# One column of a weight matrix, read at the start on GpSimd's DMA queue and not used

## The chip, the cores and the metric

The kernel runs on one core of a Trainium2 chip. A core has five engines with an instruction stream each: TensorE (PE, matmuls and transposes), VectorE (DVE), ScalarE (ACT), GpSimd (POOL) and SyncE (SP). DMAs are issued by SyncE, ScalarE and GpSimd into queues of their own, which sixteen DMA engines serve. The metric is the device time of one execution in microseconds; less is better.

## The reference

Two stages. The first is a linear recurrence over time for 4 batches x 8 heads, with states of 48 x 48; the second takes its output as 3,072 tokens of 384 numbers through two matmuls with a squared ReLU between them.

```
# r, k, v: (4, 8, 768, 48);  w, u: (8, 48)
for t in range(768):
    cur   = einsum('bhd,bhe->bhde', u * k_t, v_t)
    y_t   = einsum('bhd,bhde->bhe', r_t, state + cur)
    state = w * state + einsum('bhd,bhe->bhde', k_t, v_t)
x = y as (3072, 384)
h = x @ w_in                  # w_in:  (384, 2048)
out = max(h, 0)**2 @ w_out    # w_out: (2048, 384)
```

## The kernel before, in words

**Tiling.** Time is cut into 6 chunks of 128 steps. A unit is one chunk of one batch: 24 units, unit i = 4 x chunk + batch. Within a chunk the recurrence becomes matmuls: r and k are scaled by powers of w (step `scale`), turned so that the head dimension lies on the partitions (`turn`, `rkT` for units 0 to 5; a DMA transpose, `rkD`, from unit 6 on), multiplied with each other (`at`), masked to the lower triangle (`mask`), and multiplied by v (`y`); a diagonal term with u comes from `d` and `dv`, and the carried state from `s`, `sadd`, `sdec`, `stb`. The output of a unit, `yb`, is turned again (`xturn`, `xT`, or by DMA, `xD`), and goes through the first matmul (`m1`), ReLU and square (`relu`, `sqA` on ScalarE, `sqD` on VectorE), the second matmul (`m2`), a copy (`osb`) and a store (`out`).

**Order.** Each engine runs its instructions in the order in which the kernel writes them. That order is one long list of step names, `ORDER`; the loop at the end of the kernel walks it and calls the function of each step. A step name carries its unit, and `rt.1.1` is the second half of r of unit 1 (four heads of it). `fill.N` stands for N matmuls of a constant tile that nobody reads; they keep PE busy while it has nothing to do.

**Start.** Ahead of the list stands a prologue. ScalarE issues the loads of w, spread over partitions (`wrow`), and of half of r of unit 0; VectorE makes constants from `iota_i`, a column of partition numbers that GpSimd writes (L164); GpSimd sets the small tile `wu` and loads w and u into it (L166 to L169). The first steps of the list are then

```
kt.0.0 kt.0.1 rt.0.0 rt.1.0 I.0 rt.1.1 vt.0 ktA.1.0 lnat.0 fill.26 log@4567 kt.1.1 lnat.1 ids rt.2.0 w.1 upper w.0
fill.8 cols@1 rt.2.1 wk scale.0.0 kt.2.0 zeros scale.0.1 wr fill.8 turn.0.0@2
```

SyncE issues the halves of r and k (L281; whole pairs of units from unit 6 on, L278). GpSimd issues the four quarters of w_in (step `I`, L288, cast to bf16 on the way), v of units 0 to 5 (`vt`, L311) and the four quarters of w_out (`O`, L291), and between its first loads it builds the identity matrices (`ids`) that PE's transposes need and the mask (`upper`). PE's step `cols` (L250) turns `wu` with the small identity; behind it stand eight fills and then the first transposes of r and k (`turn`, L333).

**Waits on DMAs.** GpSimd's DMAs take eight completion semaphores in turn (named DMASW0 to DMASW7 in the rows below); the ninth DMA waits until the first has landed, and so on.

Of the kernel before, what the change touches and what calls it, by code (L numbers as in the profile page):

```python
# [8 lines left out]
F32 = mybir.dt.float32  # L9
# [74 lines left out]
def kernel(  # L84
# [11 lines left out]
    nc = tc.nc  # L96
# [12 lines left out]
    const = ctx.enter_context(tc.tile_pool(name="const", bufs=1))  # L109
# [52 lines left out]
    I32 = mybir.dt.int32  # L162
    iota_i = const.tile([128, 1], I32)
    nc.gpsimd.iota(iota_i, pattern=[[0, 1]], base=0, channel_multiplier=1)  # L164
    wu = const.tile([HP, 2, 2, 64], F32)
    nc.gpsimd.memset(wu[:, 0], 1.0)  # L166
    nc.gpsimd.memset(wu[:, 1], 0.0)
# [379 lines left out]
    def store_half(i, n):  # L547
        c, b = units[i]
        nc.sync.dma_start(out=out[b * S + c * C : b * S + (c + 1) * C, PARTS[n]], in_=tiles[i]["osb", n])

    def store(i):
        c, b = units[i]
        nc.sync.dma_start(out=out[b * S + c * C : b * S + (c + 1) * C, :], in_=tiles[i]["osb"])
# [3 lines left out]
    def names(name, *a):  # L557
# [22 lines left out]
        out=lambda i, n=None: store(i) if n is None else store_half(i, n),  # L580
# [42 lines left out]
```

## Time and profile before

| | us |
|---|---|
| median of 3 runs | 171.51 (170.11 to 173.04) |
| the profiled execution | 171.94 |
| its span, first to last instruction | 170.2 |
| PE busy | 163.9 (96%) |
| ACT busy | 129.8 (76%) |
| DVE busy | 122.3 (72%) |
| POOL busy | 15.7 (9%) |
| mean granted clock of TensorE | 0.988 |

Busy shares are over the whole span. In a row of instructions stand the start, the length, the engine, the source line, the operation, what it writes and reads, and how many; what stands in brackets is how long its engine was idle before it and what ended that. PEld is the loading of weights into PE, which overlaps the matmuls. A name like SPq or POOLq is the engine's queue of instructions, where DMAs are issued. The DMA share is the mean busy share of the sixteen DMA engines; it can pass 1, as packets of several queues overlap.

### The profile page before, as it was taken

What the parts mean: (1) busy time and instruction counts of PE and PEld (TensorE: products, weight loads), DVE (VectorE), ACT (ScalarE), POOL (GpSimd) and SP (SyncE); (2) the same over time, 40 slices, a digit from 0 to 9 for tenths busy, and PEclk for the clock granted to TensorE, in tenths of its full rate; (3) what the DMA queues carried; (4) which work ended last, traced back from release to release, by engine and by line L of the source; (5) the groups of instructions that cost most, each with busy time, mean ns of one, the idle gap of its engine ahead of it and who ended that gap; (6) DMA issues with size and microseconds to landing.
All of it is one profiled execution on the core that took longest, in us unless ns stands there. A gap on an engine that the chain in (4) does not pass through costs nothing.

```text
span 170.2 us, 4733 instructions
## 1 busy us (share of the span) xinstructions
PE 163.9 (96%) x1947; PEld 134.1 (79%) x1947; DVE 122.3 (72%) x243; ACT 129.8 (76%) x255; POOL 15.7 (9%) x36
## 2 busy tenths in 40 slices
PE   7959999999999999999999999999999999999993
PEld 7649999778787697886977887787889789688672
DVE  6567999876999989988988888989697662101100
ACT  3735999888796489698499679688699739599921
POOL 7770670000000000000000000000000000000000
PEclk9996999999999999999999999999999999999999
DMA  3999999999999899999999997998990501100044
GB/s 92 172 279 240 272 194 254 213 201 227 185 181 218 153 214 190 181 212 191 236 182 202 174 251 173 188 288 197 180 232 4 179 6 54 42 0 4 0 164 162
DMA packets 91493, 28.86 MB, mean 170 GB/s; under 512 B 82864, under 2 KB 90672, under 8 KB 91472
## 3 DMA queue, kind: packets, MB, share of 16 engines
q1 hardware_dynamic: 88416, 23.99, 67.5%
q0 software_dynamic: 2624, 4.33, 12.9%
q8 instruction: 15, 0.25, 0.6%
q10 hardware_dynamic: 432, 0.25, 0.6%
q14 instruction: 6, 0.05, 0.1%
HBM read 20.50 MB, written 4.72 MB: 148 GB/s over the span
## 4 chain that ended last, share of the span: by engine, by line
PE 87%; DMA 6%; DVE 3%; SPq 2%; issue 1%; DVEq 0%
PE bank L493 36%; PE bank L517 34%; DMA rt<-in_r_dram 4%; PE bank L369 4%; PE bank L441 3%; DMA xT<-yb 2%; PE bank L398 2%; PE bank L447 2%; SPq L281 2%; PE bank L533 2%; PE bank L333 1%; PE bank L410 1%; PE bank L345 1%; PE bank L216 1%; PE bank L477 1%
## 5 line engine op out<-in xcount | busy, mean ns | idle before, releaser
L493 PE MATMUL bank<-xT,w_in_q 128*128 128x256 bf16 (+1 forms) x720 | 72.6, 251 | 0.1
L501 ACT ACTIVATE gr<-bank 128x512 f32<-128x512 f32 x96 | 55.3, 604 | 19.0 <-PE bank L493 15.2
L517 PE MATMUL bank<-w_out_q,g 128*128 128x384 bf16 x368 | 68.6, 326 | 0.0
L493 PEld LDWEIGHTS <-w_in_q 128*128 128x128 bf16 x720 | 63.8, 113 | 3.9 <-DMA xT<-yb 0.3
L517 PEld LDWEIGHTS <-g 128*128 128x128 bf16 x368 | 34.3, 98 | 18.1 <-issue 0.2
L508 ACT ACTIVATE g<-gr 128x512 bf16<-128x512 f32 x68 | 41.2, 636 | 0.2
L377 DVE TENSOR_TENSOR am<-bank,smask 128x512 bf16<-128x512 f32 x48 | 31.3, 684 | 7.4 <-PE bank L369 6.6
L510 DVE TENSOR_TENSOR g<-gr 128x512 bf16<-128x512 f32 x28 | 19.0, 686 | 17.2 <-ACT gr L501 17.2
L524 ACT COPY osb<-bank 128x384 f32<-128x384 f32 x23 | 11.0, 480 | 5.7 <-PE bank L517 5.6
L456 DVE TENSOR_TENSOR yb<-bank,dv 128x384 bf16<-128x384 f32 x24 | 12.9, 553 | 3.2 <-PE bank L447 2.3
L420 DVE TENSOR_TENSOR dv<-vb,bank 128x384 f32<-128x384 bf16 x24 | 13.0, 548 | 2.2 <-PE bank L410 1.4
L432 ACT CAST stb<-st 128x384 bf16<-128x384 f32 x20 | 10.2, 522 | 0.6 <-DVE st L428 0.6
L301 DVE TENSOR_TENSOR rkw<-rt,wpos 128x384 bf16<-128x384 f32 x18 | 9.8, 551 | 0.8 <-DMA rt<-in_r_dram 0.7
L301 DVE TENSOR_TENSOR rkw<-kt,wneg 128x384 bf16<-128x384 f32 x18 | 9.7, 551 | 0.8 <-DMA kt<-in_k_dram 0.8
L337 ACT COPY rkT<-bank 128x512 bf16<-128x512 bf16 x12 | 7.0, 590 | 3.4 <-PE bank L333 3.4
L216 PE MATMUL bank<-warm 128*128 128x128 bf16 x87 | 8.4, 265 | 1.1 <-DVE warm L161 1.1
L441 PE MATMUL bank<-vb,am 128*128 128x48 bf16 x192 | 8.9, 185 | 0.0
L428 DVE TENSOR_TENSOR st<-st,wend 128x384 f32<-128x384 f32 x16 | 8.8, 550 | 0.0
L424 DVE TENSOR_TENSOR st<-bank,st 128x384 f32<-128x384 f32 x16 | 8.7, 549 | 0.0
L441 PEld LDWEIGHTS <-am 128*128 128x128 bf16 x192 | 7.9, 97 | 0.8
L369 PE MATMUL bank<-rkT 64*128 64x128 bf16 x192 | 8.2, 221 | 0.2 <-ACT rkT L337 0.2
L216 PEld LDWEIGHTS <-warm 128*128 128x128 bf16 x87 | 7.0, 121 | 1.2 <-DVE warm L161 1.0
(75 smaller groups left out, 120.8 us busy)
## 6 DMA issues: line engine op xcount, KB each, us to landing
out_dram<-osb SPq DMA_DIRECT2D x23, 192.0 KB, 2.4
rt<-in_r_dram SPq DMA_DIRECT2D x9, 384.0 KB, 5.8
kt<-in_k_dram SPq DMA_DIRECT2D x9, 384.0 KB, 5.2
vt<-in_v_dram SPq DMA_DIRECT2D x9, 384.0 KB, 4.5
w_in_q<-in_moe_w_in_dram POOLq DMA_DIRECT2D x4, 384.0 KB, 8.3
w_out_q<-in_moe_w_out_dram POOLq DMA_DIRECT2D x4, 384.0 KB, 8.8
vt<-in_v_dram POOLq DMA_DIRECT2D x6, 192.0 KB, 7.3
kt<-in_k_dram SPq DMA_DIRECT2D x11, 96.0 KB, 5.2
```

The costliest lines, as they stand in the source:

```text
L216: nc.tensor.matmul(out=banks[0][:, :128], lhsT=warm, rhs=warm, start=True, stop=True)
L301: nc.vector.tensor_tensor(t["rkw"][:, x, :, :, :D], pair(src), pair(wneg if x else wpos), ALU.mult)
L369: nc.tensor.matmul(out=t["at"][o][:, p, :], lhsT=t["rkT"][sl, 1, p, :], rhs=t["rkT"][sl, 0, p, :], start=True, stop=True,)
L377: nc.vector.tensor_tensor(am, t["at"][o], smask.unsqueeze(1).to_broadcast([C, HP, C]), ALU.mult)
L420: nc.vector.tensor_tensor(t["dv"], t["vb"], t["d"].unsqueeze(2).to_broadcast([C, H, D]), ALU.mult)
L441: nc.tensor.matmul(out=y[:, 2 * p + o, :], lhsT=t[f"am{o}"][:, p, :], rhs=t["vb"][:, 2 * p + o, :], start=(o == 0 and p == 0), stop=c == 0 ...
L456: nc.vector.tensor_tensor(t["yb"], t["y"], t["dv"].rearrange("p h d -> p (h d)"), ALU.add)
L493: nc.tensor.matmul(out=t["h", s][:, a], lhsT=turned, rhs=chunks[c]["xT"][:, b : b + m, n, :], start=(n == 0), stop=(n == NK - 1),)
L501: nc.scalar.activation(t["gr", s], t["h", s], AF.Relu)
L508: nc.scalar.activation(g, x, AF.Square)
L510: nc.vector.tensor_tensor(g, x, x, ALU.mult)
L517: nc.tensor.matmul(out=t["o"], lhsT=chunks[units[i][0]]["g"][:, f, units[i][1], :], rhs=w_out_q[f // 4][:, f % 4, :], start=(f == 0), stop ...
```

## The change

A tile `ahead` of one number per partition is added, and a DMA on GpSimd's queue that reads the first number of each of the first 128 rows of w_in into it. It stands between the iota and the two memsets of `wu`. Nothing reads the tile.

```
     iota_i = const.tile([128, 1], I32)
     nc.gpsimd.iota(iota_i, pattern=[[0, 1]], base=0, channel_multiplier=1)
+    ahead = const.tile([128, 1], F32)
+    nc.gpsimd.dma_start(out=ahead, in_=moe_w_in[:128, :1])
     wu = const.tile([HP, 2, 2, 64], F32)
     nc.gpsimd.memset(wu[:, 0], 1.0)
     nc.gpsimd.memset(wu[:, 1], 0.0)
```

Lines behind it count two more in the new kernel. The other engines' instructions stay as they were, in the same order. On GpSimd, at the start of its program, there stands before:

```order
L164 IOTA iota_i 128x1
L166 MEMSET wu 4x128
L167 MEMSET wu 4x128
L168 DMA wu<-in_w_dram 4x2x48 [waits Pool_49]
L169 DMA wu<-in_u_dram 4x2x48 [waits Pool_49]
L288 DMA w_in_q_147<-in_moe_w_in_dram 128x3x512
L311 DMA vt<-in_v_dram 128x8x48
```

and now:

```order
L164 IOTA iota_i 128x1
L166 DMA ahead<-in_moe_w_in_dram 128x1
L168 MEMSET wu 4x128
L169 MEMSET wu 4x128
L170 DMA wu<-in_w_dram 4x2x48 [waits Pool_49]
L171 DMA wu<-in_u_dram 4x2x48 [waits Pool_49]
L290 DMA w_in_q_149<-in_moe_w_in_dram 128x3x512
L313 DMA vt<-in_v_dram 128x8x48
```

The new DMA stands ahead of everything that GpSimd does for the rest of the kernel, behind the iota alone. Further down, where the completion semaphores come round for the first time (L311 loads v of units 1 and 2, L288 the second to fourth quarter of w_in), there stands before:

```order
L311 DMA vt<-in_v_dram 128x8x48
L288 DMA w_in_q_150<-in_moe_w_in_dram 128x3x512
L288 DMA w_in_q_149<-in_moe_w_in_dram 128x3x512
L311 DMA vt<-in_v_dram 128x8x48
L288 DMA w_in_q_148<-in_moe_w_in_dram 128x3x512 [waits DMASW0_49]
```

and now:

```order
L313 DMA vt<-in_v_dram 128x8x48
L290 DMA w_in_q_152<-in_moe_w_in_dram 128x3x512
L290 DMA w_in_q_151<-in_moe_w_in_dram 128x3x512
L313 DMA vt<-in_v_dram 128x8x48 [waits DMASW0_49]
L290 DMA w_in_q_150<-in_moe_w_in_dram 128x3x512 [waits DMASW1_49]
```

Each DMA of this queue has moved on by one semaphore: the first wait on one stands a DMA earlier, at the load of v of unit 2, and it is for the new read to have landed. The tile takes 32 bytes of each partition, so the tiles that are allocated behind it start 32 bytes further on.

More of the change, by code (lines that the diff above doesn't have):

```diff
@@ L164 @@
     nc.gpsimd.iota(iota_i, pattern=[[0, 1]], base=0, channel_multiplier=1)
+    ahead = const.tile([128, 1], F32)
+    nc.gpsimd.dma_start(out=ahead, in_=moe_w_in[:128, :1])
     wu = const.tile([HP, 2, 2, 64], F32)
```

## The prediction

> **What bounds the kernel now.** I read the head of the page first, then busy time by stretch, then the chain of waits over the start, then the timeline of the engines that stand in it.
>
> ```profile
> span 170.2 us, 4733 instructions
> ...
> PE 163.9 (96%) x1947; PEld 134.1 (79%) x1947; DVE 122.3 (72%) x243; ACT 129.8 (76%) x255; POOL 15.7 (9%) x36
> ...
> 0.00:10.00 10.00, 7.54 (x86) 6.25 (x86) 5.06 (x22) 5.04 (x9) 8.11 (x25) 1.00 0.74 163
> 10.00:20.00 10.00, 9.05 (x148) 8.29 (x149) 8.60 (x17) 6.20 (x15) 3.10 (x6) 0.83 1.15 244
> 20.00:160.00 140.00, 139.94 (x1658) 114.44 (x1656) 108.33 (x204) 115.24 (x226) 4.47 (x7) 1.00 0.83 167
> ```
>
> The last three rows give a stretch, then busy time of PE, PEld, DVE, ACT and POOL, then the granted clock, the DMA share and GB/s. From 20 to 160 us PE is busy 139.94 of 140 us at full clock: the middle is PE's and one small DMA cannot shorten it. What is open lies before 20 us: PE is idle there for 3.4 us, and the clock averages 0.83 from 10 to 20.
>
> The chain of waits over that start (start, length, what):
>
> ```profile
> 3.02 0.61 SPq L281
> ...
> 3.67 6.36 DMA rt<-in_r_dram
> ...
> 12.40 0.61 PE bank L333 x4
> ```
>
> SyncE issues loads of r and k; the last half of r's second unit (step rt.1.1) is in flight until 10.03; VectorE scales it, TensorE turns it, and from 12.4 on the chain is nearly all PE. **So the time is the moment at which r's second unit has come, plus what follows at PE's pace.** The change acts on GpSimd's queue, which isn't in this chain, but feeds it at two places: the identity for PE's first transposes, and transfers beside r's.
>
> **What it adds on GpSimd.** Its timeline:
>
> ```profile
> 1.56 0.76 POOL L168 DMA_DIRECT2D wu<-in_w_dram  x1 [0.31 <-POOL wu L167]
> ...
> 2.32 0.62 POOL L169 DMA_DIRECT2D wu<-in_u_dram  x1
> ...
> 2.94 0.82 POOL L288 DMA_DIRECT2D w_in_q<-in_moe_w_in_dram  x1
> ...
> 3.72 0.96 POOL L311 DMA_DIRECT2D vt<-in_v_dram  x1
> ...
> 5.21 0.29 POOL masks.py:199 TENSOR_SCALAR_AFFINE_SELECT identb<-identb 128x128 bf16<-128x128 bf16 x1
> ```
>
> A DMA that GpSimd issues occupies it: 0.62 us (8 rows) to 0.96 us (1,024 rows). The new one has 128 rows and is the first; I take 0.76, the row of today's first. The bounds are 0.62 and 0.96, plus up to 0.31 if it starts with a gap like the one ahead of L168. So everything behind moves by 0.6 to 1.3 us, taken 0.76: L288's first quarter from 2.94 to 3.7, vt.0 from 3.72 to 4.5, identb's end from 5.50 to 6.26. The lane semaphores of this queue turn by one, so the third load of v (issued at 10.1) now waits for the new read; that landed long before (wu took 2.4 us, below), so this costs nothing.
>
> Who waits for the identity:
>
> ```profile
> 5.59 0.20 PEld L250 LDWEIGHTS bank<-ident,wu 4*128 4x128 f32 x2 [0.20 <-POOL identb masks.py:199]
> ...
> 6.49 0.87 PE L333 MATMUL bank<-identb,rkw 128*128 128x128 bf16 x8
> ...
> 8.65 0.24 PE L389 MATMUL bank<-uwb,rk 128*128 128x8 bf16 x4
> ...
> 10.13 0.56 DVE L303 TENSOR_TENSOR rkw<-rt,wfour 128x384 bf16<-128x384 f32 x1 [1.63 <-DMA rt<-in_r_dram]
> ...
> 10.74 0.40 PE L333 MATMUL bank<-identb,rkw 128*128 128x128 bf16 x4 [1.84 <-DVE rkw L303]
> ```
>
> L250 goes from 5.59 to 6.35, and with eight fills behind it the first transposes start near 7.2 instead of 6.49. The whole first unit moves with them: its diagonal sums (L389) end near 9.6 instead of 8.89. Behind them stands a wait of 1.84 us on PE, and 1.63 us on DVE, for rt.1.1. **So this part is priced at 0: that wait hides it.** Cover left: 1.1 us. If it were gone, 0.76 would go straight to the end.
>
> The queue's other loads also come later, against these landings and uses:
>
> ```profile
> wu<-in_w_dram POOLq DMA_DIRECT2D x1, 1.5 KB, 2.4
> ...
> vt<-in_v_dram POOLq DMA_DIRECT2D x1, 192.0 KB, 7.5
> ...
> w_in_q<-in_moe_w_in_dram POOLq DMA_DIRECT2D x1, 384.0 KB, 9.2
> ...
> 8.58 1.52 POOL L288 DMA_DIRECT2D w_in_q<-in_moe_w_in_dram  x2
> ...
> 11.66 0.52 ACT L318 CAST vb<-vt 128x384 bf16<-128x384 f32 x1
> ...
> 12.80 0.53 PE L441 MATMUL bank<-vb,am 128*128 128x48 bf16 x8
> ...
> 19.64 1.50 PE L493 MATMUL bank<-xT,w_in_q 128*128 128x128 bf16 x24
> ```
>
> The last number of a DMA row is the time from issue to landing. vt.0 lands at 3.72 + 7.5 = 11.2 and is cast from 11.66 to 12.18; PE uses it at 12.80: 0.46 us of cover ahead of the cast and 0.6 behind it, 1.06. The quarter of w_in issued second in the row of two (8.58 + half of 1.52 = 9.34) lands 9.2 later, at 18.5, and is used at 19.64: 1.1 us. Both covers hold 0.76 even if each landing moves by all that its issue does; neither holds 1.3.
>
> **What it takes away.** Packets by DMA queue (q1 is SyncE's, q0 GpSimd's; packets, MB, share of 16 engines). The first row is the stretch 3.0 to 3.5 us, the second 3.5 to 4.5, the first pair 4.5 to 5.5, the last pair 5.5 to 6.5:
>
> ```profile
> q0 software_dynamic: 27, 0.00, 3.7%
> ...
> q1 hardware_dynamic: 233, 0.16, 68.3%
> ...
> q0 software_dynamic: 26, 0.03, 56.0%
> q1 hardware_dynamic: 29, 0.02, 7.8%
> ...
> q0 software_dynamic: 89, 0.09, 54.8%
> q1 hardware_dynamic: 83, 0.06, 33.8%
> ```
>
> From 4.5 on w_in's first packets stand in q0, and 26 of them hold 56% of 16 engines for 1 us: 16 x 0.56 / 26 = 0.34 us each. A us later it is 16 x 0.548 / 89 = 0.10 us each. Something in the first touch of w_in costs some 26 x 0.24 = 6.3 engine-us, 0.4 us on each of 16 engines, and unevenly; meanwhile SyncE's queue falls from 233 packets to 29, while rt.1.0 and rt.1.1 are under way. The new read touches 128 of w_in's 384 rows. wu's packets (first row) come some 1.5 to 1.9 us behind its issue at 1.56, so the new read, issued near 1.1, gets to memory around 2.8 us. Only wrow, k's and r's first unit are then in flight, and all of the first unit has the 1.1 us of cover named above. So it can move the stall away from rt.1.1, and w_in's first quarter itself comes 0.76 us later. Bounds for rt.1.1: nothing gained, even 0.5 lost, if the stall only moves up and holds back r's and k's first halves; at best the whole poor microsecond, 1.0, which the 1.1 us of cover above would let through. A third of the rows are touched, and the row nearest to a price is the 0.4 us mean per engine. I take 0.5 gained.
>
> **The clock.** Four neighbouring stretches of equal length, columns as above:
>
> ```profile
> 5.60:9.02 3.42, 2.99 (x45) 2.26 (x44) 1.57 (x4) 2.42 (x6) 2.62 (x9) 1.00 1.11 239
> 9.02:12.44 3.42, 1.49 (x24) 1.33 (x25) 2.31 (x5) 1.31 (x3) 2.73 (x4) 0.99 1.10 277
> 12.44:15.86 3.42, 3.42 (x43) 3.03 (x44) 2.29 (x5) 1.13 (x3) 0.00 (x0) 0.51 1.17 220
> 15.86:19.28 3.42, 3.42 (x71) 3.21 (x69) 3.28 (x8) 3.36 (x9) 0.62 (x2) 1.00 1.17 253
> ```
>
> After a stretch with PE busy 1.49 of 3.42 us the clock is halved for 3.42 us; after one with 2.99 it is not. The half clock costs at most 1.7 us of PE time, less what waits for ACT and DVE anyhow; I estimate 1.0. With unit 0 later and rt.1.1 earlier, PE would be busy some 2.1 to 2.6 us of the second stretch: between the two rows, so undecided. I count 0 and keep -1.0 as an end. [...]
>
> **Sum**, against the profiled execution (171.94 us, of it 1.74 outside the span): 0.76 hidden, -0.5 at rt.1.1, 0 for the clock: 171.4. That execution was 0.43 above the median of the runs shown, 171.51; from the median the sum gives 171.0. I forecast 171.2, own range 170.3 to 172.1: chance 0.48.
>
> **Rivals.**
> 1. *The gap closes.* rt.1.1 comes 1.0 earlier and the half clock is gone: 171.5 - 2.0 = 169.5. For it: 29 packets against 233. Against: two thirds of w_in's rows stay untouched. Chance 0.22, a quarter of it in a tail beyond 2%.
> 2. *GpSimd's lateness comes through.* The new read's stall only moves, rt.1.1 stays at 10.03, and vt.0 or a quarter of w_in lands too late: +0.8 to +1.3, 172.3 to 172.8. It decides from a delay of 1.0 on vt.0. Chance 0.17.
> 3. *Slower all along, through addresses.* The new tile takes 32 bytes of each partition, so every later tile starts 32 bytes further on.
>
> ```profile
> q1 hardware_dynamic: 77414, 18.26, 92.6%
> ...
> rt<-in_r_dram SPq DMA_DIRECT2D x9, 384.0 KB, 5.8
> ...
> DVE rkw L301 <- DMA kt<-in_k_dram: 0.8, 2, 0.5
> DVE rkw L301 <- DMA rt<-in_r_dram: 0.7, 1, 0.7
> ```
>
> The first row is 20 to 120 us: 16 engines x 92.6 us / 77,414 = 19 ns a packet. The 27 pair loads (9 each of r, k and v) write 55,296 rows of 192 bytes; should such a packet take longer, it decides from about 7%, the share that this queue leaves free there. I price 10%, my choice: 55,296 x 1.9 ns / 16 = 6.6 us of DMA time. DVE already waits 1.5 us for such loads and PE for none, so I price what gets through at half, +3: 174.5. Against it: nothing in the trace tells tiles apart by address. Chance 0.13. [...]
>
> **The chances.** The range reaches from 169.2 (rival 1 with a little scatter) to 173.4 (rival 2 and the mild end of rival 3), and leaves out some 0.18. Runs of the kernel before spread over 1.7%, so 2% is what can be told from no change. Faster by over 2% (under 168.1): 0.06, the tail of rival 1. Slower by over 2% (over 174.9): 0.10, most of it rival 3. Within: 0.84.
>
> **What would show it.** In the new profile: L250 near 6.35 and the transposes near 7.2; DVE's wait for rt shorter and ending near 9.5; SyncE's queue with well over 29 packets in the microsecond in which w_in's quarter begins; PE busy from 20 to 160 us as now. I am wrong if PE waits in the middle of the run, if vt.0 or w_in is what PE's first matmuls wait for, or if more than one stretch of half clock appears.

## The result, and the profile after

The changed kernel takes **172.69 us** (median of 20 runs, 171.71 to 173.72), the kernel before 170.87 in the same comparison (20 runs). The ratio is 1.0104 [1.0082, 1.0127]: **slower by 1.8 us**, less than the 2% bound, but well outside the interval. I had forecast 171.2 and no change or a small gain. The time lies above the inner range (170.3 to 172.1) and inside the outer one (169.2 to 173.4); the direction is wrong. The sum had also started too high, from 171.51, the median of three runs, where twenty give 170.87. The profiled execution of the changed kernel took 171.74 us.

The head of its page, and of the section on queues the row of SyncE's queue (packets, MB, share of 16 engines):

```profile
span 169.9 us, 4734 instructions
...
PE 162.8 (96%) x1947; PEld 132.9 (78%) x1947; DVE 122.6 (72%) x243; ACT 130.2 (77%) x255; POOL 16.4 (10%) x37
...
PEclk9999999999999999999999999999999999999999
...
q1 hardware_dynamic: 88416, 23.99, 74.8%
```

The same row of the kernel before:

```profile
q1 hardware_dynamic: 88416, 23.99, 67.5%
```

The same packets and the same bytes take 11% more DMA time. This execution shows no stretch of half clock (granted 1.000 over the whole), and the profile of before did (0.988 over the whole, 0.51 from 12.44 to 15.86 us). A second profile of the unchanged kernel shows none either (granted 1.0; its span is 169.0 us, against 170.2 with it), so the half clock comes and goes without the change, and the fair partner of a profile at full clock is this one of 169.0.

The stretches that the prediction began with, in the profile after:

```profile
0.00:10.00 10.00, 8.02 (x103) 6.91 (x104) 6.58 (x25) 5.50 (x10) 8.49 (x26) 1.00 0.74 166
10.00:20.00 10.00, 8.06 (x144) 6.87 (x141) 8.52 (x17) 6.88 (x17) 5.30 (x8) 1.00 1.16 239
20.00:160.00 140.00, 139.71 (x1649) 114.15 (x1648) 107.24 (x201) 114.75 (x224) 2.66 (x5) 1.00 0.91 167
```

and in the second profile of before:

```profile
0.00:10.00 10.00, 7.16 (x90) 5.94 (x91) 5.84 (x24) 5.03 (x9) 8.03 (x25) 1.00 0.73 168
10.00:20.00 10.00, 9.17 (x167) 8.08 (x165) 9.27 (x19) 7.92 (x18) 5.17 (x9) 1.00 1.15 237
20.00:160.00 140.00, 139.87 (x1646) 114.22 (x1643) 106.85 (x201) 115.13 (x225) 2.55 (x5) 1.00 0.82 167
```

Up to 10 us PE is ahead with the change (103 matmuls, against 86 and 90 before); in the second stretch it falls behind (144, against 148 and 167, and the 148 with a third of the stretch at half clock). In the long middle PE is idle for 0.29 us, against 0.06 and 0.13, and the DMA share is 0.91 where it was 0.83 and 0.82.

The timeline of the start, of GpSimd and of those whom it feeds:

```profile
1.34 0.68 POOL L166 DMA_DIRECT2D ahead<-in_moe_w_in_dram  x1 [0.39 <-issue]
...
2.52 0.62 POOL L170 DMA_DIRECT2D wu<-in_w_dram  x1 [0.17 <-POOL wu L169]
...
5.82 0.28 PE L252 MATMUL bank<-ident,wu 4*128 4x4 f32 x2 [0.59 <-POOL ident masks.py:199]
...
6.57 0.81 PE L335 MATMUL bank<-identb,rkw 128*128 128x128 bf16 x8
...
8.44 0.55 DVE L305 TENSOR_TENSOR rkw<-rt,wfour 128x384 bf16<-128x384 f32 x1
...
11.30 0.51 ACT L320 CAST vb<-vt 128x384 bf16<-128x384 f32 x1 [1.23 <-DMA vt<-in_v_dram]
```

The load of w is 0.96 us later (1.56 before). r's second half no longer holds anything up: VectorE scales it at 8.44 without a wait (10.13 before, 9.18 in the second profile of before). But ScalarE now waits 1.23 us for v, and PE waits for other things. PE's waits over the whole run (total, times, longest), without the first row, 1.1 us for the constant that the fills read, which is there before too:

```profile
...
PE bank L495 <- DMA w_in_q<-in_moe_w_in_dram: 0.7, 1, 0.7
PE bank L252 <- POOL ident masks.py:199: 0.6, 1, 0.6
PE bank L443 <- ACT vb L320: 0.6, 1, 0.6
PE bank L335 <- DVE rkw L305: 0.4, 1, 0.4
PE bank L495 <- DMA xT<-yb: 0.2, 1, 0.2
...
```

The 1.84 us for `rkw` have become four smaller waits. The last row shown is new in kind: PE waits in the middle of the run, at 80 us, for a DMA transpose of y on SyncE's queue. I had named that as a sign of being wrong.

### The profile page after: what moved, and what is told of

Read it like the earlier page. It is cut to its first block, busy times and chain, and to the rows that moved or that the text cites. A ratio compares the mean times of both kernels' runs of the same rounds, so it can differ in the third digit from the quotient of the medians.

```text
span 169.9 us, 4734 instructions
## 1 busy us (share of the span) xinstructions
PE 162.8 (96%) x1947; PEld 132.9 (78%) x1947; DVE 122.6 (72%) x243; ACT 130.2 (77%) x255; POOL 16.4 (10%) x37
## 3 DMA queue, kind: packets, MB, share of 16 engines
q1 hardware_dynamic: 88416, 23.99, 74.8%
## 4 chain that ended last, share of the span: by engine, by line
PE 80%; DMA 11%; POOL 4%; DVE 2%; issue 1%; POOLq 0%; DVEq 0%
PE bank L495 35%; PE bank L519 32%; DMA w_in_q<-in_moe_w_in_dram 5%; DMA xT<-yb 5%; PE bank L371 3%; PE bank L443 2%; PE bank L449 2%; PE bank L400 2%; PE bank L535 2%; POOL vt L313 1%; PE bank L412 1%; PE bank L335 1%; POOL w_in_q L290 1%; PE bank L347 0%; DVE rkw L303 0%
## 5 line engine op out<-in xcount | busy, mean ns | idle before, releaser
L218 PE MATMUL bank<-warm 128*128 128x128 bf16 x87 | 7.5, 246 | 1.1 <-DVE warm L161 1.1
L371 PEld LDWEIGHTS <-rkT 64*128 64x128 bf16 x192 | 5.5, 94 | 3.1 <-issue 2.0
```

The costliest lines, as they stand in the source:

```text
L371: nc.tensor.matmul(out=t["at"][o][:, p, :], lhsT=t["rkT"][sl, 1, p, :], rhs=t["rkT"][sl, 0, p, :], start=True, stop=True,)
```

## The experiments

**Two theories.** *Lateness*: GpSimd's queue starts later, and v and w_in come too late. *Addresses*: the 32 bytes of the new tile put the tiles behind it off the multiples of 256 bytes on which the loads of r, k and v wrote, and SyncE's queue becomes slower all along.

**1. One without the other.** `late_read` keeps the tile and the read, but issues it as the last of GpSimd's loads, at 23 us:

```
+    ahead = const.tile([128, 1], F32)
...
+        if what == "O.3":
+            nc.gpsimd.dma_start(out=ahead, in_=moe_w_in[:128, :1])
```

> The same read and the same tile at the same place in memory, but issued as the last DMA of GpSimd's program (near 25 us), so that all tiles are shifted by 32 bytes as in the changed kernel and nothing on GpSimd is late. Theory A (lateness): as the kernel before, ratio 0.997 to 1.003. Theory B (addresses): as the changed kernel, ratio near 1.010.

Measured: 1.0082 [1.0052, 1.0112], queue 74.5%. `busy_instead` has neither tile nor read; one memset is written eight times and keeps GpSimd busy:

```
-    nc.gpsimd.memset(wu[:, 0], 1.0)
+    for _ in range(8):
+        nc.gpsimd.memset(wu[:, 0], 1.0)
```

> No read and no new tile: GpSimd writes the same small constant seven times more ahead of its loads of w and u (some 0.14 us each, 1.0 us), so that everything behind is as late as in the changed kernel, at the old addresses. Theory A (lateness): as the changed kernel, ratio 1.007 to 1.013. Theory B (addresses): as before, ratio 0.997 to 1.003. Theory C (the read itself: w_in is touched early, SyncE's loads overtake GpSimd's): as before too, and r's second unit lands at 10 us rather than at 8.4.

Measured: 1.0093 [1.0057, 1.0129], queue 66.3%. It was overdosed: the load of w came at 3.18, 1.62 us late instead of 1.0, beyond the cover of 1.1 us, and PE waited 1.3 us for the small identity. So both mechanisms can cost 0.9%, and this run doesn't tell what 0.78 to 0.96 us of lateness cost. The changed kernel and the kernel before, once more in the same comparison:

> The changed kernel once more, unchanged, for a second profile; its first one (171.74 us) is one of its fastest executions, its median is 172.69. Theory A (GpSimd's issues come later, so w_in's quarters and v land later and PE's first matmuls wait for them): in a typical execution PE waits 1.5 to 2.5 us in all for w_in and v before 25 us, and is busy without a gap behind that. Theory B (every later tile starts 32 bytes further on and DMAs are slower all along): PE waits after 25 us too, or DMA time per packet of SyncE's queue from 20 to 120 us is above the 19.1 ns of before.

> The kernel before once more, unchanged, for a second profile. Its first profile (171.94 us) has a half clock from 12.4 to 15.9 us, and its median is 170.87. If the half clock made that execution slow, this profile has none, its span is some 1 us shorter (about 169.2), and PE's first matmul on the third quarter of w_in (step m1.0.2, at 19.64 before) starts near 18.6, close to that quarter's landing at 18.5. If the half clock is the rule, it is seen again and the span is near 170.

Measured: 1.0094 [1.0049, 1.0138] for the change, queue 73.4%; 0.9987 [0.9959, 1.0014] for the kernel before, queue 67.7%.

**2. The lateness at its own size, and other shifts.** `aligned_read` is the change with a tile of 256 bytes, so that every tile stands where it stood modulo 256; GpSimd's lateness stays. `r_read` is the same, but reads a column of r and leaves w_in untouched. `shift64` is `late_read` with 64 bytes. The percentages in what was expected of it are the share of SyncE's queue.

```
-    ahead = const.tile([128, 1], F32)
-    nc.gpsimd.dma_start(out=ahead, in_=moe_w_in[:128, :1])
+    ahead = const.tile([128, 64], F32)
+    nc.gpsimd.dma_start(out=ahead[:, :1], in_=moe_w_in[:128, :1])
```

> The changed kernel with its read where it is, but the tile is 256 bytes wide, so that every later tile keeps its place against multiples of 256. Left of the change: GpSimd's lateness and the early touch of w_in. Lateness and addresses as two causes that add: SyncE's queue back at 67%, no wait of PE from 60 to 100 us, ratio 1.003 to 1.007 (the changed kernel less the 0.65 us that the shifted kernels lose between 72 and 84 us). Addresses alone: ratio 0.997 to 1.003. Lateness alone: ratio near 1.010.

> As the read with the tile 256 bytes wide, but the column comes from r (unit 0's rows, which SyncE loads anyhow), so that w_in isn't touched early and GpSimd is as late. If the early touch of w_in gives something back, this is slower than the read of w_in by 0.3 to 0.8 us and r's second unit lands at 9.5 to 10 us. If only lateness counts, both are the same within 0.3 us and r's second unit lands near 8.4 in both.

> As the late read, but the tile is 64 bytes wide, so that all later tiles start 64 bytes further on instead of 32. [...] Theory B2 (any move off a multiple of 256 costs): 73 to 75% and a ratio near 1.008. Theory B3 (the late read itself costs, not the addresses): 67% and a ratio near 1.008.

Measured: `aligned_read` 1.0007 [0.9978, 1.0035], queue 67.0%; `r_read` 1.0015 [0.9985, 1.0046], 66.1%; `shift64` 0.9976 [0.9947, 1.0004], 68.9%. With the change's own lateness and no displacement no loss shows: **the lateness costs between -0.2% and 0.5%, the displacement of `late_read` about 0.8%.** Nor does every displacement cost: with 64 bytes neither the time nor the queue (68.9%, against 67.5% and 67.7% in the profiles of before) shows a loss like that with 32. That w_in's rows are touched beforehand is worth nothing that can be measured either.

The half clock blurs this comparison. A granted clock under 0.995 over the whole execution, as a stretch of half clock leaves it (0.988 in the first profile of before), stands in 17 of the 35 executions of the kernel before, and in 1 of 12 of `aligned_read` and of `r_read`. Among the others the medians are 170.93, 171.28 and 171.18. So at equal clock the lateness seems to cost some 0.2%, from 11 executions each: a small part of the loss rather than none. `late_read` at equal clock stands at 172.13 against 170.55, 0.9%.

What became of the half of r that comes earlier is seen in PE's waits of `aligned_read`, where its transposes no longer wait for `rkw`:

```profile
PE bank L495 <- DMA w_in_q<-in_moe_w_in_dram: 1.7, 2, 1.1
```

In the profile of before PE waited 2.0 us for `rkw` and not measurably for w_in. Once PE comes earlier, w_in, which is issued 0.78 us later, is the next wait, of 1.7 us.

`swap` asked whether v could be had earlier for nothing, by issuing vt.0 ahead of w_in's first quarter in the kernel before:

```
-kt.0.0 kt.0.1 rt.0.0 rt.1.0 I.0 rt.1.1 vt.0
+kt.0.0 kt.0.1 rt.0.0 rt.1.0 vt.0 rt.1.1 I.0
```

> The kernel before, without the read, with two of GpSimd's DMAs exchanged: v of unit 0 is issued ahead of the first quarter of w_in. In the changed kernel ScalarE waits 1.2 us for that v. If v's landing is what holds the start once r is early, v lands some 1.5 us earlier and the ratio is 0.994 to 0.998; if w_in's third quarter, issued far behind both, sets the start, nothing changes: 0.998 to 1.002.

Measured: 1.0023 [0.9992, 1.0055]; no gain.

**3. Which tiles it is.** `loads_only` puts an unused tile of 32 bytes at the end of the constants and one of 224 at the end of the loads' pool: only the tiles that receive r, k and v are displaced. `rest_only` displaces everything else and leaves these where they were.

```
loads_only, before the pool of the loads and in step vt.0:
+    pad0 = const.tile([128, 8], F32, name="pad0", bufs=1)
...
+        if what == "vt.0":
+            pad1 = loads.tile([128, 56], F32, name="pad1", bufs=1)
rest_only, ahead of wu, before the pool of the loads, and in step vt.0:
+    pad0 = const.tile([128, 8], F32, name="pad0", bufs=1)
...
+    pad1 = const.tile([128, 56], F32, name="pad1", bufs=1)
...
+        if what == "vt.0":
+            pad2 = loads.tile([128, 8], F32, name="pad2", bufs=1)
```

> Before with two unused tiles, of 32 bytes at the end of const and of 224 bytes at the end of loads: only the tiles that the loads of r, k and v write stand 32 bytes further, and w_in_q, w_out_q, rkw, rkT, xT and the rest where they stood before. Nothing is read or timed otherwise (two one-column memsets on GpSimd at O.3 give the tiles a writer). Theory that the 192-byte rows of the loads make the change slower: the whole loss, 1.006 to 1.011 of before (about 172.5 us), and SyncE's queue at 73 to 75 % of the span instead of 67.5 %. Theory that the DMA transposes or the loads of w_in and w_out make it: 1.000, and SyncE's queue at 66 to 69 %.

> The other half: an unused tile of 32 bytes ahead of wu, and padding that puts the tiles of the loads of r, k and v back on multiples of 256, while rkw, w_in_q, w_out_q, rkT, xT and all work tiles stand 32 bytes further, as in the changed kernel. Theory that the load rows make it: 0.998 to 1.003 (about 171 us), SyncE's queue 66 to 69 %. Theory that transposes, w_in or operands of the engines make it: 1.006 to 1.011, and the queue over 72 %.

Measured: `loads_only` 1.0088 [1.0058, 1.0118], `rest_only` 0.9994 [0.9958, 1.0029]. Their rows for SyncE's queue, first `loads_only`:

```profile
q1 hardware_dynamic: 88416, 23.99, 73.1%
```

and `rest_only`:

```profile
q1 hardware_dynamic: 88416, 23.99, 67.9%
```

Both give their unused tiles a writer by memsets of one column on GpSimd at step O.3, which the excerpts above leave out. Nothing is read in `loads_only` and nothing is late, and its loss can't be told from the change's (1.0104 and 1.0094): **32 bytes under the destinations of the loads are the cause** of all or nearly all of it. Where matmul operands, w_in, w_out, `rkw` and the transposes' destinations stand makes no difference that shows.

The packets of 192 bytes on this queue say what happens to them (40 to 110 us, counted from the trace):

```
run           loads' place   packets   up to 16 ns   17-40 ns (mean)   over 40 ns   mean
b_again          0 mod 256    41,334      98%          2% (23.6)          0.3%      15.4 ns
rest_only        0 mod 256    41,012      99%          1% (25.4)          0.2%      15.4 ns
shift64         64 mod 256    41,303      97%          3% (22.9)          0.3%      15.5 ns
loads_only      32 mod 256    42,219      82%         18% (25.6)          0.3%      17.2 ns
late_read2      32 mod 256    42,724      78%         22% (25.1)          0.2%      17.5 ns
shift96b        96 mod 256    42,849      80%         20% (25.6)          0.2%      17.5 ns
shift160       160 mod 256    41,947      76%         23% (25.7)          0.2%      17.8 ns
```

The rows of 192 bytes lie end to end, so a tile's rows start at four places modulo 256, which are the same four with a displacement of 64 as with none. Displaced by 32, about one row in five takes 25 ns instead of 15, and the others are as fast as before. The last two lines belong to the next runs.

**4. Which displacements, and through which wait.** `shift96` and `shift160` are `late_read` with tiles of 96 and 160 bytes.

> The read late in GpSimd's order, with a tile of 96 bytes instead of 32, so that all tiles behind it stand 96 bytes further. Theory that places off a multiple of 64 bytes are the slow ones: as with 32 bytes, 1.006 to 1.011, queue 73 to 75 %. Theory that only 32 of 256 is bad (or that the distance from a multiple of 128 counts otherwise): 0.998 to 1.003, queue 66 to 69 %.

Measured: 1.0012 [0.9983, 1.0041], queue 72.9%. That was a surprise: the rows are as slow as with 32 bytes, and the time is not. So these were run beside each other:

> The late read with the tile of 32 bytes once more, beside the next three on one chip. If its loss is the chip-independent one: 1.005 to 1.011 and the queue at 73 to 75 %.

> The tile of 96 bytes once more, beside that of 32. Theory that the time follows the slowness of the load rows alone: as late_read2 within 0.2 % (the queue at 73 %, rows slow alike). Theory that it takes the transposes' lateness as well, which 96 bytes did not show: 0.998 to 1.004, 0.4 to 0.8 % under late_read2.

> The same with a tile of 160 bytes, so that the loads' tiles stand 160 past a multiple of 256 (32 past one of 128). Theory that only the remainder by 64 counts: the queue at 73 to 75 % as with 32 and 96; and in time as one of those two. Theory that the remainder by 256 counts: the queue between 66 and 72 %.

Measured: `late_read2` 1.0141 [1.0080, 1.0202], queue 73.6%; `shift96b` 1.0029 [0.9996, 1.0061], 73.1%; `shift160` 1.0089 [1.0054, 1.0123], 74.4%. `late_read2` is the kernel of `late_read`, which had 1.0082; their intervals overlap. All three slow the queue; 32 and 160 cost 0.8 to 1.4%, 96 much less. At equal clock (0.995 or more) 96 bytes cost something too: medians of 171.37 and 171.56 against 170.87 and 170.61, and 173.24 for `late_read2` beside the second. The stretch from 65 to 130 us (PE, PEld, DVE, ACT, POOL, clock, DMA share, GB/s) in the second profile of before:

```profile
65.00:130.00 65.00, 65.00 (x751) 53.38 (x749) 56.70 (x108) 53.68 (x104) 0.00 (x0) 1.00 1.00 195
```

in `late_read2`:

```profile
65.00:130.00 65.00, 63.79 (x715) 51.40 (x714) 56.19 (x106) 51.95 (x100) 0.00 (x0) 1.00 1.10 199
```

in `shift160`:

```profile
65.00:130.00 65.00, 63.41 (x712) 51.11 (x711) 55.65 (x105) 51.92 (x101) 0.00 (x0) 1.00 1.12 199
```

and in `shift96b`:

```profile
65.00:130.00 65.00, 64.92 (x734) 52.69 (x733) 56.77 (x107) 53.50 (x104) 0.00 (x0) 1.00 1.08 199
```

With 32 and 160 bytes PE falls 1.2 to 1.6 us short here; the two profiles of the changed kernel, whose times (171.74 and 172.21) lie under its median, have 64.71 and 64.75. The stretches are cut by time and not by the program. From the start of PE's 300th matmul to that of its 1,900th, counted from the traces:

```
loads not displaced, or by 64 (9 profiles)            138.1 to 138.5 us
the changed kernel (2)                                138.8, 138.9
96 bytes: shift96, shift96b                           138.8, 138.8
32 bytes: late_read, loads_only, late_read2           139.0, 139.1, 140.1
160 bytes: shift160                                   140.5
```

Every displacement that slows the queue costs time here, 96 bytes no less than the changed kernel in its own profiles. `aligned_read` and `r_read`, which have the lateness alone, stand at 138.1, and `busy_instead` at 138.5, so what the lateness costs lies before this.

In the middle PE waits for a step behind the loads on the same queue. SyncE's issues around 80 us in the second profile of before:

```profile
71.81 0.42 SPq L278 DMA_DIRECT2D kt<-in_k_dram  x1
...
75.11 2.18 SPq L467 DMA_TRANSPOSE xT<-yb  x1
```

and in `late_read`, with PE's wait, which ends when these transposes have landed (75.81 and 4.4 to landing):

```profile
73.21 0.42 SPq L279 DMA_DIRECT2D kt<-in_k_dram  x1
...
75.81 2.45 SPq L468 DMA_TRANSPOSE xT<-yb  x1
...
80.27 1.50 PE L494 MATMUL bank<-xT,w_in_q 128*128 128x256 bf16 x12 [0.25 <-DMA xT<-yb]
```

PE stood level with before up to here (0.15 us apart at 36 and at 74 us); the queue is 0.7 us later with the transposes `xT`, and PE waits. Over 30 to 130 us the transposes `rkT` took 5.9 us from issue to landing (median) in the second profile of before, 6.5 to 7.3 in the profiles with 32 and 160 bytes, and 5.8 and 6.0 with 96; with 64 bytes, which cost no time, they took 6.5. So this goes some way with the loss, but doesn't explain it.

Waits of PE for `xT` in the middle come to 0.2 to 0.3 us in the two profiles of the changed kernel and in `late_read`, to 0.6 in `loads_only`, 1.0 in `late_read2` and 1.2 in `shift160`; the profiles with 96 bytes and those without displacement have none that shows.

`xt_first` is `late_read` with one load of r moved behind the transposes that followed it on the queue:

```
-sadd.9 sqA.6.1 y.9@3 rt.14 y.8@4 ... sdec.9 xD.8 m1.6.4@6
+sadd.9 sqA.6.1 y.9@3 y.8@4 ... sdec.9 xD.8 rt.14 m1.6.4@6
```

> late_read with one step moved in the order: the load of r for chunk pair 14 is issued behind the transposes xT of pair 8 on SyncE's queue instead of ahead of them (the ones that PE waits for at 80 us in the displaced kernels). Theory that this wait carries the second part of the loss (0.6 us): 0.996 to 0.998 of late_read2, so 1.002 to 1.008 of before. Theory that the loss would only go to the next wait: as late_read2 within 0.2 %, or slower through the later r.

Measured: 1.0131 [1.0072, 1.0189], beside 1.0141 for `late_read2`. Of its waits on PE:

```profile
...
PE bank L494 <- DMA w_in_q<-in_moe_w_in_dram: 0.9, 2, 0.6
PE bank L494 <- DMA xT<-yb: 0.6, 2, 0.3
PE bank L518 <- DVE g L511: 0.4, 1, 0.4
...
PE bank L442 <- DVE am L378: 0.3, 1, 0.3
...
```

The edit reached other transposes than I meant. Those of `xD.8` go out at 65.06 us in `late_read2`, and PE waits for them at 70; in `xt_first` they go out at 63.60, and that wait is gone. Those that PE waits for at 80 us are the next ones, `xD.10`, which still stand behind two loads:

```profile
74.57 2.22 SPq L279 DMA_DIRECT2D rt<-in_r_dram  x1
...
76.88 2.49 SPq L468 DMA_TRANSPOSE xT<-yb  x1
...
81.31 1.50 PE L494 MATMUL bank<-xT,w_in_q 128*128 128x256 bf16 x12 [0.32 <-DMA xT<-yb]
```

In `late_read2` that wait was 0.28. So what the wait at 80 us is worth was not tried. The one at 70 us (0.30 in `late_read2`) is gone without a gain that shows; two others, for `am` at 73 us and for `g` at 80, are new.

**5. A better place?** `rkw256` moves only the `rkw` tiles, which the transposes read, from 160 past a multiple of 256 onto one, with unused tiles of 96 bytes ahead and 160 behind:

```
+    pad0 = const.tile([128, 24], F32, name="pad0", bufs=1)
     rkw_b = [const.tile([128, 2, 2, HP, 2, 64], BF16, name=f"rkw{n}") for n in range(NPAD)]
...
+    pad1 = const.tile([128, 40], F32, name="pad1", bufs=1)
```

> Before with 96 unused bytes ahead of the rkw tiles and 160 behind, so that rkw, whose rows of 256 bytes the DMA transposes read, stand on multiples of 256 instead of 160 past one, and the tiles behind rkw where they stood modulo 256. Theory that rows off a multiple of 64 cost only where a load writes them: 1.000, queue as before at 67.5 %. Theory that the transposes' rows cost by the same rule, in reading too: the queue's share falls to 62 to 65 % and the kernel is 0.5 to 1 us faster, 0.994 to 0.997.

Measured: 0.9971 [0.9938, 1.0005], queue 66.0%. The queue is at most slightly shorter, and a gain of 0.3% is not shown: the interval reaches 1. The same holds for `shift64`. No version beat the kernel before.

## Why the prediction was wrong, point by point

- **What bounds the kernel**: the start and PE's pace, "one small DMA cannot shorten" the middle. True of the read, but what the tile does to the middle was looked for only in a rival. There PE's 300th to 1,900th matmul take 138.8 and 138.9 us with the change, against 138.4 and 138.5. The DMA share of 0.83 there stood in the quoted row.
- **GpSimd's lateness, taken 0.76**: 0.96 at the load of w (1.56 to 2.52) and 0.78 at w_in and at v (2.94 to 3.72, 3.72 to 4.50). Inside the bounds. L252 ran only 0.23 us later, not 0.76: it waits for the small identity, which is ready before the large one that the bracket named; the transposes came 0.08 later, at 6.57.
- **Hidden, priced at 0**: right to within half a per cent, though the wait for r that was to hide it is gone in the changed kernel. `aligned_read` and `r_read` have all of the lateness and lose nothing that shows over all executions, some 0.2% (0.3 us) at equal clock; `busy_instead`, with 1.62 us against a cover of 1.1, loses 0.9%.
- **-0.5 at r's second half**: this term of the sum was wrong. The half came earlier than my best end: it landed at 7.83 and 7.55 in the two profiles with the change, against 10.03 and 9.09 before, and VectorE scaled it at 8.44. The reason was not the touch of w_in that I gave: `r_read` doesn't touch it and has 8.22. What goes with it is when w_in's first quarter is issued. In the twelve profiles that issue it at 2.9 the half lands between 8.73 and 10.10; in `swap`, which touches nothing early and issues the quarter at 3.85 (with v ahead of it), at 8.24; with the change's lateness (3.72) between 7.35 and 8.22; in `busy_instead` (4.55) at 6.57. SyncE's queue moves 172 packets from 4.5 to 5.5 us in the changed kernel, 212 in `r_read` and 184 in `busy_instead`, where before had 29 (104 in its second profile). And the gain came to nothing: I had spent one cover twice. The 1.1 us of cover at w_in (and 1.06 at v) were counted with PE at its old pace, and the earlier r draws on them too. In the changed kernel PE waits 0.7 us for w_in and 0.6 for the cast of v, in `aligned_read` 1.7 for w_in.
- **The clock at 0**: the end at -1.0 came nearer than I had it. None of 27 executions of the changed kernel has a granted clock under 0.995; 39 of 118 of the kernel before, over the four later comparisons, have, and their medians are 0.7 to 1.3 us above the others'. By these counts the missing half clock is worth some 0.3 us on average, which the loss exceeds. That the change removed it is not shown: `late_read` has it in 5 of 12, but so few as 1 of 12 have it in `shift64`, which isn't late.
- **Addresses, chance 0.13, priced at +3**: this is what happened, and **counting it at 0 in the sum is the step that failed**; `loads_only` has 1.0088 by it alone. "Nothing in the trace tells tiles apart by address" was no evidence against it, since all the loads' tiles of before stood at the same place. The size: rows took 17.5 instead of 15.4 ns, +14% where I priced 10%, my choice, for which no run before it had a figure; that is 55,296 x 2.1 ns / 16 = 7.3 us of DMA time against my 6.6. The whole queue's time grew by 12 us (74.8% of 169.9 against 67.5% of 170.2), since the transposes' packets of 256 bytes in it also became slower (28 ns against 25 to 26 on average, from 40 to 110 us). Of this 1.4 to 1.5 us reached the end in `late_read` and `loads_only` and 2.4 in `late_read2`, where I took half of 6.6. Nor is 100% a limit of the share, as I had it with the 7% left free: over 20 to 120 us it went from 92.6% to 103.6%, and from 40 to 110 us this queue alone had 103.7% before.

**What stays open**: why rows at 32, 96 and 160 bytes are slower and at 64 are not, for which no run shows a mechanism; and why 96 bytes slow the rows as 32 do and cost less time. Both its profiles have a stretch of reduced clock at the start, so that at 36 us PE is 0.9 to 1.4 us behind the second profile of before, which may give the queue a lead. That alone can't be it, since at equal clock 96 bytes still stand at 171.56 beside 173.24. And 96 bytes move more than the loads: they put `rkw` from 160 past a multiple of 256 onto one, the very move that `rkw256` made alone (0.9971, queue 66.0%), and the transposes `rkT`, which read it, took 5.8 and 6.0 us. A gain there may offset part of the loss; no run displaces the loads by 96 and leaves `rkw` where it was.

## What to carry to other kernels

A new tile is a change to the address of every tile allocated behind it: before pricing its traffic, list which DMA destinations it displaces and by how much (here 32, 96 and 160 bytes raised the queue's share from 67.5% to between 72.9% and 74.8%, 64 and 256 left it at 68.9% and 67.0%), and if a queue is as busy as this one (92.6% from 20 to 120 us), pad the tile (here to 64 bytes, 0.9976, or to 256, 1.0007) instead of arguing. When two effects come early in a program, price them against the same cover once: here the half of r that came earlier left PE waiting 0.7 us for w_in in the changed kernel and 1.7 in `aligned_read`. A small experiment that keeps the displacement and drops the traffic, and one that does the opposite, settle most of such a case in two runs; and before moving a step to test a wait, check in the trace that it is the step of that wait.

## What the runs showed that I had not expected

- Loads of 192-byte rows into tiles 32, 96 or 160 bytes past a multiple of 256 slow a queue by 8 to 11%, and only about one row in five is slower (25 ns for 15).
- Equal slowness of the rows does not mean equal time: 1.0141 with 32 bytes and 1.0029 with 96, side by side.
- A kernel's median mixes executions with and without a stretch of half clock, which lie 0.7 to 1.3 us apart; the 0.2% that the lateness seems to cost shows only among executions of equal clock.
- One memset of 4 partitions repeated seven times more delayed GpSimd's queue by 1.62 us, where the change's own DMA delayed it by 0.96.
